# Spreading softmax reciprocals over partitions: by PE matmuls, or through DRAM and by DMA from batch 2 on

## The chip, the cores and the metric

One core of a Trainium2 chip. The time is the device time of one execution in microseconds (us); medians of several executions are given. Engines: PE (matmuls), DVE (vector), ACT (activations), POOL (here it issues the loads) and SP (here it issues output stores, transposes and, in the changed kernel, the row transfers). The 16 DMA engines carry all transfers.

## The reference

Attention over 8 batches, 12 heads, 448 positions, head size 64, then a gated projection pair over the heads' outputs put side by side:

```python
scores = scale * np.matmul(q, k.transpose(0, 1, 3, 2))
scores = scores - np.max(scores, axis=-1, keepdims=True)
attn = np.exp(scores)
attn = attn / (np.sum(attn, axis=-1, keepdims=True) + 1e-09)
attn_out = np.matmul(attn, v)
...  # [batch, heads, seq, 64] -> x [batch * seq, heads * 64]
h = x @ w_in          # 768 x 2048
g = h * np.cos(h)
return g @ w_out      # 2048 x 768
```

## The kernel before

Everything works on transposed tiles: a head's 64 values lie on partitions, its 448 query positions along the free dimension. One step `S` makes scores, `AV` multiplies the exponentials with the values (tile `asb`, not yet normalized), `DN` gets the sums of the exponentials by matmuls with ones (`den`), `N` takes their reciprocals, `R` spreads the reciprocals over the 64 partitions of each head and multiplies, `H` is the first projection (`hps`), `O` the second (`ops`). A sum lies on one partition per head and half of the positions, and it is wanted on 64; `R` does this by a matmul with an indicator matrix:

```python
    def R(ck, b, c):                        # c: one of 3 groups of 4 heads
        ...
        for j in range(2):
            for qh_ in range(2):
                nc.tensor.matmul(rps[j][:, ts(qh_, SH)], ind[:, 2 * c + j, qh_, :, :], rhl[b],
                                 start=True, stop=True)
        ...
        nc.vector.tensor_tensor(out=xt, in0=asb[b, c], in1=both[:, :, 0:S_], op=ALU.mult)
```

The order of PE is fixed when the kernel is built. A planner with a clock of its own (`weave`) takes the next step of the batch if its inputs should be ready, else a step of the next batch ("ahead"), else a piece of the output projection of the batch before ("fill"):

```python
    AHEAD, LATE, KEEP = 3, 6, 8
    ...
        ahead = nxt[: AHEAD if b else 4]
        weave([body, ahead], keep, LATE)
        weave([scaled(b), ahead], keep)                                 # R, R, H, ...
        weave([[(H, b, f2) for f2 in range(2, NFC // 2)]], keep)
        fill += [(O, b, tt, nh, [i, i + 1]) ...]
```

Whenever its buffers should be free, the planner also runs `W`, two DVE copies of the next loaded q and k (which free the load buffer, so POOL starts the next load), and `X`, a DMA transpose of the copy on SP's queue.

The softmax here doesn't subtract the row's maximum and nothing guards it: scores larger than these inputs give would overflow.

Of the kernel before, what the change touches and what calls it, by code (L numbers as in the profile page):

```python
# [11 lines left out]
FP = mybir.dt.float32  # L12
F16 = mybir.dt.float16
AF = mybir.ActivationFunctionType
ALU = mybir.AluOpType
# [56 lines left out]
def kernel(  # L72
# [9 lines left out]
    nc = tc.nc  # L82

    B, NH, S_, D = q.shape
# [17 lines left out]
    sb = ctx.enter_context(tc.tile_pool(name="sb", bufs=2))  # L102
    big = ctx.enter_context(tc.tile_pool(name="big", bufs=1))
    ps = ctx.enter_context(tc.tile_pool(name="ps", bufs=1, space=bass.MemoryType.PSUM))



# [60 lines left out]
    lowrow = const.tile([P, 1], FP, name="lowrow")  # L168
    ind = const.tile([P, NP, 2, 2, D], F16, name="ind")
    halfpi = const.tile([P, 1], FP, name="halfpi")  # L170
    zero = const.tile([P, 512], F16, name="zero")

    def emit_consts_vector():
        nc.vector.memset(zero, 0.0)
# [40 lines left out]
    def take(ck, tag, among=None):  # L215
        return ck.free(tag, among)
# [169 lines left out]
    def DN(ck, b, cs, rs=range(NR)):  # L386
# [16 lines left out]
        for c in cs:  # L403
            for r in rs:
                for h in range(2):
                    for qh_ in range(2):
# [6 lines left out]
                            stop=(c == NQ - 1 and r == NR - 1),  # L413
                        )

    def N(ck, b):
        tag, at = ck.ready["den slot", b]
        ck.slots[tag][at] = ck.on_dve(ck.ready["den", b], 1.5)
        ck.ready["rhl", b] = ck.on_dve(0.0, 0.6)
        if ck is not clk:  # L420
            return
        rr = sb.tile([P, SH], FP, name="rr", tag="rr", bufs=1)
        nc.vector.reciprocal(out=rr, in_=den[b])  # L423
        hi = sb.tile([P, SH], F16, name="hi", tag="hi", bufs=1)
        nc.vector.tensor_copy(out=hi, in_=rr)
        t = sb.tile([P, SH], F16, name="rhl", tag="rhl", bufs=1)
        rhl[b] = t
        nc.vector.scalar_tensor_tensor(
            out=t, in0=hi, scalar=lowrow, in1=rr, op0=ALU.mult, op1=ALU.subtract
        )  # L430

    def R(ck, b, c):

# [38 lines left out]
    def H(ck, b, f2, cs=range(NQ)):  # L472


        if cs[0] == 0:
            ck.ready["hps", f2], t = take(ck, "big", None)
            ck.need(max(t, arrive["win", f2 // 2]))
            if f2 == 0:
                ck.ready["gT slot", b], t = take(ck, "gT", None)
                ck.ready["gT free", b] = t  # L480
        for c in cs:
            ck.need(ck.ready["xT", b, c])
            end = ck.mm("full", 4, 0.189)
        last = cs[-1] == NQ - 1
        at = ck.ready["hps", f2]
        if last:
            if f2 == NFC // 2 - 1:
                for c in range(NQ):
                    ck.slots["xT"][ck.ready["xT slot", b, c]] = ck.pe
            t = ck.on_act(end, 1.0, "sin")  # L490
            t = ck.on_dve(max(t, ck.ready["gT free", b]), 1.09)
            ck.slots["big"][at] = ck.ready["gT", b, f2] = t
        if ck is not clk:
            return
        if f2 == cs[0] == 0:
            gT[b] = big.tile([P, NFC, S_], F16, name="gT", tag=f"gT{ck.ready['gT slot', b]}")
        if cs[0] == 0:
            hpss[f2] = ps.tile([P, 2, 512], FP, name="hps", tag=f"big{at}")
        for i in range(2):
            for kc in range(2 * cs[0], 2 * cs[-1] + 2):  # L500
                nc.tensor.matmul(  # L501
                    hpss[f2][:, i, 0:S_],
                    w_in16[:, kc, ts(2 * f2 + i, P)],
                    xT[b, kc // 2][:, kc % 2, :],
                    start=(kc == 0),
                    stop=(kc == NKC - 1),
                )
        if not last:
            return
        cos = sb.tile([P, 2, S_], FP, name="cs", tag="cs")  # L510
        nc.scalar.activation(out=cos, in_=hpss[f2][:, :, 0:S_], func=AF.Sin, bias=halfpi)  # L511
        nc.vector.tensor_tensor(  # L512
            out=gT[b][:, 2 * f2 : 2 * f2 + 2, :],
            in0=cos,
            in1=hpss[f2][:, :, 0:S_],
            op=ALU.mult,
        )
# [4 lines left out]
    def O(ck, b, tt, nh, fcs):  # L522


        rest = tt == NT
        wait = max(ck.ready["gT", b, fc // 2] for fc in fcs)
        ck.need(max(wait, arrive["wout", 1 if rest else nh]))
        if fcs[0] == 0:
            ck.ready["ops slot"], t = take(ck, "m", None)
            ck.need(t)  # L530
        at = ck.ready["ops slot"]
        end = ck.mm("col64" if rest else "full", len(fcs), 0.1625)
        last = fcs[-1] == NFC - 1
        if last:
            ck.slots["m"][at] = ck.on_act(end, 0.48) if nh == 0 else ck.on_dve(end, 0.556)
            if rest:
                ck.slots["gT"][ck.ready["gT slot", b]] = end
        if ck is not clk:
            return
        gt = gT[b]  # L540
        if fcs[0] == 0:
            opss[0] = ps.tile([P, EH], FP, name="ops", tag=f"m{at}")
        ops = opss[0]
        for fc in fcs:
            for half in (0, 1) if rest else (nh,):
                nc.tensor.matmul(  # L546
                    ops[64 * half : 64 * half + 64, :] if rest else ops,
                    gt[:, fc, ds(P * tt, 64 if rest else P)],
                    w_out16[:, fc, ts(half, EH)],
                    start=(fc == 0),  # L550
                    stop=(fc == NFC - 1),
                )
        if not last:
            return
        osb = sb.tile([P, EH], FP, name="osb", tag="osb", bufs=5)
        (nc.scalar.copy if nh == 0 else nc.vector.tensor_copy)(out=osb, in_=ops)  # L556
        dst = out.rearrange("(b p r) (n e) -> b r n p e", b=B, r=NR, n=2)
        for i in range(2):
            to = dst[b, NR - 1, i] if rest else dst[b, 2 * tt + i, nh]
            nc.sync.dma_start(out=to, in_=osb[SP * i : SP * i + SP, :])  # L560
# [14 lines left out]
    def transpose_ahead():  # L575

        while to_transpose:
            b, c = to_transpose[0]
            now = max(clk.pe, clk.dve)
            if zeros and b > 0:  # L580
                return
            if arrive.get(("qk", b, c), LATER) > now - (1.0 if b and c else 0.0) or min(clk.slots["qkp"]) > now or min(clk.slots["qkT"]) > now:
                return
            to_transpose.pop(0)
            run((W, b, c))
            if b > 1:
                run((X, b, c))
            else:
                soon.extend([(T, b, c, 1), (T, b, c, 0)])

    def weave(lists, keep, late=99):



        body = lists[0]
        while body:
            transpose_ahead()
            waits = []
            todos = ([body, soon] if zeros else [soon, body])
            for todo in todos + (lists[1:] if len(body) <= late else []):  # L600
                while todo and todo[0][0] is N:
                    run(todo.pop(0))
                if todo:
                    w = stall(todo[0])
                    if w <= SLACK:
                        run(todo.pop(0))
                        break
                    waits.append((w, todo))
            else:
                if len(fill) > keep:  # L610
                    waits.append((stall(fill[0]), fill))
                least = min(waits, key=lambda x: x[0])[0] if waits else 1e9
                if zeros and least > 0.15:
                    run((Z,))
                elif least > 1e6:
                    clk.pe += 0.1
                else:
                    run(min(waits, key=lambda x: x[0])[1].pop(0))
# [14 lines left out]

    def scaled(b):

        tail = [(R, b, 0), (R, b, 1), (H, b, 0, [0]), (R, b, 2), (H, b, 0, [1])]
        return tail + [(H, b, 1, [0, 1]), (H, b, 0, [2]), (H, b, 1, [2])]

    LATER = 1e9
    SLACK = 0.02  # L640
    AHEAD, LATE, KEEP = 3, 6, 8
    ctx.enter_context(tc.manual_schedule(engines=None))


# [37 lines left out]
    for b in range(B):  # L682
        nxt = attention(b + 1) if b + 1 < B else []
        ahead = nxt[: AHEAD if b else 4]
        keep = KEEP if b > 0 else 0
        weave([body, ahead], keep, LATE)
        weave([scaled(b), ahead], keep)
        weave([[(H, b, f2) for f2 in range(2, NFC // 2)]], keep)
        halves = [(tt, nh) for tt in range(NT) for nh in range(2)]
        if b == 0:  # L690
            halves.sort(key=lambda x: x[1])
        fill += [(O, b, tt, nh, [i, i + 1]) for tt, nh in halves for i in range(0, NFC, 2)]
        fill += [(O, b, NT, 0, range(i, i + 8)) for i in range(0, NFC, 8)]
        body = ahead + nxt[AHEAD if b else 4 :]
    for step in fill:
        run(step)
# [30 lines left out]
```

## Time and profile before

| | before |
|---|---|
| time, median | 429.27 us (429.02 to 429.66) |
| PE busy | 98% |
| idle notes on PE's timeline, all batches | 3.7 us, all but 0.5 in the first 34 us |
| `rps` matmuls (the spreading) | 96, four per group, 0.385 us a group |

The prediction shows the engine table, the chain and PE's timeline behind one batch's sums. To these belong the longest entries of the list of what PE waited for (engine, line, what ended the wait: us in total, times, longest):

```profile
PE z L229 <- DVE onehot L177: 1.2, 1, 1.2
PE sc L330 <- ACT qkT L299: 1.0, 1, 1.0
PE hps L501 <- DVE xT L463: 0.5, 1, 0.5
```

The steady batches give PE nothing to wait for. The third line, in batch 2, is the only one of a later batch; the three entries left out (0.5, 0.3 and 0.2 us) lie in the first 34 us.

### The profile page before, as it was taken

Reading aid. Unit: us, or ns where it says so; the run is one execution under the profiler, and the core shown is the slowest. Engines: PE = TensorE matmul, PEld = TensorE weight load, DVE = VectorE, ACT = ScalarE, POOL = GpSimd, SP = SyncE. Lnnn points to the kernel's source line nnn. Section 1 sums busy time; section 2 is a strip of 40 time slices with the busy share of each in tenths; the row PEclk is TensorE's granted clock in tenths of the full one; section 3 lists DMA queues with packets and bytes.
Section 4 is the critical chain, followed back from the end, with each engine's and each line's share of the span. In section 5 each row is a group of like instructions: output and inputs, shape, how many; then the busy total and the mean of one; then the engine's idle time right before and its main releaser. Section 6 shows DMA issues by size and latency. Waiting matters only on the chain.

```text
span 427.3 us, 9170 instructions
## 1 busy us (share of the span) xinstructions
PE 419.1 (98%) x4027; PEld 223.8 (52%) x4027; DVE 171.6 (40%) x237; ACT 242.0 (57%) x286; POOL 68.6 (16%) x103
## 2 busy tenths in 40 slices
PE   8989999999999999999999999999999999999995
PEld 3435545655455554655546554555546555565563
DVE  3335633654235542354226442355413542165310
ACT  4898386356755457545774457554575547614300
POOL 7785224101220022100320012100000000000000
PEclk9999999999999999999999999999999999999999
DMA  9999999992996059920999009720364001120033
GB/s 194 191 164 199 204 211 191 163 142 43 177 153 85 0 80 197 127 54 1 137 180 139 2 20 204 149 40 2 73 114 78 20 2 37 40 55 2 18 76 74
DMA packets 68871, 43.12 MB, mean 101 GB/s; under 512 B 36064, under 2 KB 68832, under 8 KB 68832
## 3 DMA queue, kind: packets, MB, share of 16 engines
q0 software_dynamic: 26496, 22.35, 37.2%
q1 hardware_dynamic: 42064, 19.74, 24.9%
q8 instruction: 31, 0.51, 0.5%
q10 hardware_dynamic: 272, 0.46, 0.3%
q14 instruction: 8, 0.07, 0.0%
HBM read 45.61 MB, written 11.01 MB: 133 GB/s over the span
## 4 chain that ended last, share of the span: by engine, by line
PE 88%; DMA 6%; POOL 3%; issue 1%; DVE 1%; ACT 0%; POOLq 0%
PE hps L501 34%; PE ops L546 33%; PE sc L330 8%; PE av L366 7%; DMA win<-in_moe_w_in_dram 4%; PE den L408 3%; DMA out_dram<-osb 2%; PE rps L453 2%; POOL win L155 1%; POOL qkn L133 1%; POOL ind L202 1%; POOL vn L143 1%; DVE osb L556 0%; PE tp L296 0%; ACT osb L556 0%
## 5 line engine op out<-in xcount | busy, mean ns | idle before, releaser
L339 ACT ACTIVATE pT<-sc 128x896 f16<-128x896 f32 x168 | 142.4, 930 | 61.5 <-PE sc L330 61.4
L546 PE MATMUL ops<-wout,gT 128*128 128x384 f16 (+1 forms) x1024 | 162.1, 327 | 0.0
L501 PE MATMUL hps<-xT,win 128*128 128x448 f16 x768 | 148.2, 352 | 0.5 <-DVE xT L463 0.5
L546 PEld LDWEIGHTS <-gT 128*128 128x128 f16 (+1 forms) x1024 | 83.1, 101 | 70.4 <-issue 25.4
L511 ACT ACTIVATE cs<-hps,halfpi 128x896 f32<-128x896 f32 x64 | 63.6, 1006 | 84.3 <-PE hps L501 84.3
L501 PEld LDWEIGHTS <-win 128*128 128x128 f16 x768 | 74.6, 98 | 68.7 <-DVE xT L463 1.6
L512 DVE TENSOR_TENSOR gT<-cs,hps 128x896 f16<-128x896 f32 x64 | 68.9, 1087 | 77.0 <-ACT cs L511 77.0
L378 DVE COPY asb<-av 128x896 f32<-128x896 f32 x23 | 25.1, 1092 | 70.6 <-PE av L366 70.6
L330 PE MATMUL sc<-qkT 64*64 64x448 f16 x672 | 45.5, 359 | 1.0 <-ACT qkT L299 1.0
L556 DVE COPY osb<-ops 128x384 f32<-128x384 f32 x24 | 13.3, 555 | 68.4 <-PE ops L546 53.1
L366 PE MATMUL av<-pT,vn 64*64 64x448 f16 x672 | 38.9, 353 | 0.0
L133 POOL DMA_DIRECT2D qkn<-in_q_dram x23 | 16.6, 723 | 125.6 <-DVE qkp L243 121.9
L143 POOL DMA_DIRECT2D vn<-in_v_dram x24 | 17.2, 717 | 122.1 <-PE av L366 121.0
L556 ACT COPY osb<-ops 128x384 f32<-128x384 f32 x32 | 15.9, 496 | 29.8 <-DMA out_dram<-osb 18.0
L330 PEld LDWEIGHTS <-qkT 64*64 64x64 f16 x672 | 16.2, 105 | 24.2 <-issue 20.3
L463 DVE TENSOR_TENSOR xT<-asb,rps 128x896 f16<-128x896 f32 x21 | 22.2, 1085 | 9.4 <-PE rps L453 9.3
L366 PEld LDWEIGHTS <-vn 64*64 64x64 f16 x672 | 17.6, 106 | 15.1 <-issue 5.9
L408 PE MATMUL den<-pT,onehot 128*32 128x224 f16 x672 | 18.1, 260 | 0.0
L133 POOL DMA_DIRECT2D qkn<-in_k_dram x23 | 16.6, 723 | 6.7 <-DMA wout<-in_moe_w_out_dram 5.3
L408 PEld LDWEIGHTS <-onehot 128*32 128x32 f16 x672 | 15.3, 97 | 3.8 <-issue 3.8
L423 DVE RECIPROCAL rr<-den 128x224 f32<-128x224 f32 x8 | 12.5, 1557 | 11.9 <-PE den L408 11.9
L243 DVE COPY qkp<-qkn 128x896 f16<-128x896 f16 x46 | 15.7, 388 | 0.1
(34 smaller groups left out, 110.9 us busy)
## 6 DMA issues: line engine op xcount, KB each, us to landing
out_dram<-osb SPq DMA_DIRECT2D x112, 96.0 KB, 2.3
vn<-in_v_dram POOLq DMA_DIRECT2D x24, 224.0 KB, 6.3
qkn<-in_q_dram POOLq DMA_DIRECT2D x23, 224.0 KB, 6.6
qkn<-in_k_dram POOLq DMA_DIRECT2D x23, 224.0 KB, 8.9
win<-in_moe_w_in_dram POOLq DMA_DIRECT2D x16, 192.0 KB, 8.3
wout<-in_moe_w_out_dram POOLq DMA_DIRECT2D x2, 1536.0 KB, 19.0
stage<-in_k_dram ACTq DMA_DIRECT2D x1, 448.0 KB, 4.9
stage<-in_q_dram SPq DMA_DIRECT2D x1, 448.0 KB, 4.6
```

What stands on the lines that cost most here:

```text
L133: nc.gpsimd.dma_start(out=t[:, i], in_=rows_of(src, b, c))
L330: nc.tensor.matmul(sc[lo, h, 0:S_], t[64 * h : 64 * h + 64, 1, r, lo], t[64 * h : 64 * h + 64, 0, :, lo], start=True, stop=True,)
L339: nc.scalar.activation(out=pT[b, c][:, r, :, :], in_=sc[:, :, 0:S_], func=AF.Exp, scale=scale)
L366: nc.tensor.matmul(avs[c][64 * h : 64 * h + 64, j, 0:S_], vn[64 * j : 64 * j + 64, h, ts(r, D)], p[64 * j : 64 * j + 64, r, h, :], start=( ...
L378: copy(out=a, in_=avs[c][:, :, 0:S_])
L408: nc.tensor.matmul(den[b][32 * g : 32 * g + 32, :], onehot[:, c, :], pT[b, c][:, r, h, ts(qh_, SH)], start=(c == 0 and r == 0), stop=(c == ...
L463: nc.vector.tensor_tensor(out=xt, in0=asb[b, c], in1=both[:, :, 0:S_], op=ALU.mult)
L501: nc.tensor.matmul(hpss[f2][:, i, 0:S_], w_in16[:, kc, ts(2 * f2 + i, P)], xT[b, kc // 2][:, kc % 2, :], start=(kc == 0), stop=(kc == NKC ...
L511: nc.scalar.activation(out=cos, in_=hpss[f2][:, :, 0:S_], func=AF.Sin, bias=halfpi)
L512: nc.vector.tensor_tensor(out=gT[b][:, 2 * f2 : 2 * f2 + 2, :], in0=cos, in1=hpss[f2][:, :, 0:S_], op=ALU.mult,)
L546: nc.tensor.matmul(ops[64 * half : 64 * half + 64, :] if rest else ops, gt[:, fc, ds(P * tt, 64 if rest else P)], w_out16[:, fc, ts(half, ...
L556: (nc.scalar.copy if nh == 0 else nc.vector.tensor_copy)(out=osb, in_=ops)
```

## The change

Its intent is to take `R` off the busiest engine. From batch 2 on, the reciprocals (fp32) are written to DRAM, and each head's row is read back to all 64 partitions of that head; then DVE multiplies with that (`M`). More work of other batches is kept for the time that this takes, and no new transposes are put on SP's queue shortly before the rows.

```diff
+    BY_DMA = 2
     def N(ck, b):
...
         nc.vector.reciprocal(out=rr, in_=den[b])
+        if b >= BY_DMA:
+            rows = dram.tile([2, 32, 2, SH], FP, name="rows", tag="rows")
+            for h in range(2):
+                nc.sync.dma_start(
+                    out=rows[h].rearrange("m q x -> q m x"), in_=rr[64 * h : 64 * h + 64])
+            for c in range(NQ):
+                rb[b, c] = sb.tile([P, 2, S_], FP, name="rb", tag="cs", bufs=3)
+                for h in range(2):
+                    row = rows[h, 2 * c : 2 * c + 2].rearrange("m q x -> (m q x)")
+                    nc.sync.dma_start(
+                        out=rb[b, c][64 * h : 64 * h + 64].rearrange("p j x -> p (j x)"),
+                        in_=row.unsqueeze(0).to_broadcast([64, 2 * S_]))
+            return
...
+    def M(ck, b, c):
+        nc.vector.tensor_tensor(out=xT[b, c], in0=asb[b, c], in1=rb[b, c], op=ALU.mult)
...
-        osb = sb.tile([P, EH], FP, name="osb", tag="osb", bufs=5)
+        osb = sb.tile([P, EH], FP, name="osb", tag="osb", bufs=4)
...
-            transpose_ahead()
+            if not (body[0][0] in (AV, DN, N) and body[0][1] >= BY_DMA and len(body) <= 3):
+                transpose_ahead()
...
-    AHEAD, LATE, KEEP = 3, 6, 8
+    AHEAD, LATE, KEEP = 5, 7, 28
+    LAND = 8.0
```

Cut: the planner's bookkeeping, its rule that output pieces also fill a wait of over 0.3 us, the new order behind the sums (`M` and one group's part of `H` in turn, then the rest of `H`), the third buffer of tag `cs`, the memory of `zero` shared with another tile, and the half output of a batch as one step in place of two.

More of the change, by code (lines that the diff above doesn't have):

```diff
@@ L104 @@
     ps = ctx.enter_context(tc.tile_pool(name="ps", bufs=1, space=bass.MemoryType.PSUM))
+    dram = ctx.enter_context(tc.tile_pool(name="dram", bufs=2, space=bass.MemoryType.DRAM))
     clk = Clock({"big": 3, "m": 2, "pT": 4, "qkp": 3, "qkT": 4, "asb": 4, "xT": 3, "gT": 2})
@@ L170 @@
     halfpi = const.tile([P, 1], FP, name="halfpi")
-    zero = const.tile([P, 512], F16, name="zero")
+    zero = big.tile([P, 512], F16, name="zero", tag="pT3")
     def emit_consts_vector():
@@ L414, in DN @@
                         )
+    BY_DMA = 2
+    rb = {}
     def N(ck, b):
         tag, at = ck.ready["den slot", b]
-        ck.slots[tag][at] = ck.on_dve(ck.ready["den", b], 1.5)
-        ck.ready["rhl", b] = ck.on_dve(0.0, 0.6)
+        ck.slots[tag][at] = t = ck.on_dve(ck.ready["den", b], 1.5)
+        if b < BY_DMA:
+            ck.ready["rhl", b] = ck.on_dve(0.0, 0.6)
+        else:
+            for c in range(NQ):
+                ck.ready["rb", b, c] = t + LAND + 1.5 * c
         if ck is not clk:
@@ L423, in N @@
         nc.vector.reciprocal(out=rr, in_=den[b])
+        if b >= BY_DMA:
+            rows = dram.tile([2, 32, 2, SH], FP, name="rows", tag="rows")
+            for h in range(2):
+                nc.sync.dma_start(
+                    out=rows[h].rearrange("m q x -> q m x"), in_=rr[64 * h : 64 * h + 64]
+                )
+            for c in range(NQ):
+                rb[b, c] = sb.tile([P, 2, S_], FP, name="rb", tag="cs", bufs=3)
[3 more added lines that the diff above has]
+                        out=rb[b, c][64 * h : 64 * h + 64].rearrange("p j x -> p (j x)"),
+                        in_=row.unsqueeze(0).to_broadcast([64, 2 * S_]),
+                    )
+            return
         hi = sb.tile([P, SH], F16, name="hi", tag="hi", bufs=1)
@@ L430, in N @@
         )
+    def M(ck, b, c):
+        at, t = take(ck, "xT", None)
+        t = max(t, ck.ready["rb", b, c])
+        if ck is not clk:
+            return ck.need(t)
+        ck.ready["xT", b, c] = ck.on_dve(t, 1.09)
+        ck.slots["asb"][ck.ready["asb slot", b, c]] = ck.ready["xT", b, c]
+        ck.ready["xT slot", b, c] = at
+        xT[b, c] = sb.tile([P, 2, S_], F16, name="xT", tag=f"xT{at}", bufs=1)
+        nc.vector.tensor_tensor(out=xT[b, c], in0=asb[b, c], in1=rb[b, c], op=ALU.mult)
     def R(ck, b, c):
@@ L481, in H @@
         for c in cs:
-            ck.need(ck.ready["xT", b, c])
+            ck.need(ck.ready.get(("xT", b, c), LATER))
             end = ck.mm("full", 4, 0.189)
@@ L509, in H @@
             return
-        cos = sb.tile([P, 2, S_], FP, name="cs", tag="cs")
+        cos = sb.tile([P, 2, S_], FP, name="cs", tag="cs", bufs=3)
         nc.scalar.activation(out=cos, in_=hpss[f2][:, :, 0:S_], func=AF.Sin, bias=halfpi)
@@ L609, in weave @@
             else:
-                if len(fill) > keep:
+                least = min(waits, key=lambda x: x[0])[0] if waits else 1e9
+                if len(fill) > keep or fill and least > 0.3:
                     waits.append((stall(fill[0]), fill))
-                least = min(waits, key=lambda x: x[0])[0] if waits else 1e9
+                    least = min(least, waits[-1][0])
                 if zeros and least > 0.15:
@@ L634, in scaled @@
     def scaled(b):
+        if b >= BY_DMA:
+            tail = []
+            for c in range(NQ):
+                tail += [(M, b, c), (H, b, 0, [c])]
+            return tail + [(H, b, 1)]
         tail = [(R, b, 0), (R, b, 1), (H, b, 0, [0]), (R, b, 2), (H, b, 0, [1])]
@@ L686 @@
         weave([body, ahead], keep, LATE)
+        keep = 0
         weave([scaled(b), ahead], keep)
@@ L692 @@
         fill += [(O, b, tt, nh, [i, i + 1]) for tt, nh in halves for i in range(0, NFC, 2)]
-        fill += [(O, b, NT, 0, range(i, i + 8)) for i in range(0, NFC, 8)]
+        fill.append((O, b, NT, 0, range(NFC)))
         body = ahead + nxt[AHEAD if b else 4 :]
```

## The prediction

> **What bounds the kernel now.** I read the page's engine table first, then the chain that ended last, then the PE part of the timeline around one batch's softmax sums, and last the DMA views. The engine table and the chain say the same thing:
>
> ```profile
> PE 419.1 (98%) x4027; PEld 223.8 (52%) x4027; DVE 171.6 (40%) x237; ACT 242.0 (57%) x286; POOL 68.6 (16%) x103
> ...
> PE 88%; DMA 6%; POOL 3%; issue 1%; DVE 1%; ACT 0%; POOLq 0%
> ```
>
> PE is busy for 98% of the span and carries 88% of the chain; the other engines have over 40% to spare. A busy PE need not be a dense one, so I checked the timeline. After batch 2 it shows no idle note on PE at all. A batch is 50.0 us long (the sums of batch 5 end at 277.7 us, those of batch 6 at 327.75). The stretch behind the sums of batch 6 is where the change works:
>
> ```profile
> 325.62 2.20 PE L408 MATMUL den<-pT,onehot 128*32 128x224 f16 x84
> 327.75 1.47 PE L546 MATMUL ops<-wout,gT 128*128 128x384 f16 x8
> 329.15 0.76 PE L330 MATMUL sc<-qkT 64*64 64x448 f16 x12
> 329.85 1.15 PE L546 MATMUL ops<-wout,gT 128*128 128x384 f16 x6
> 330.83 0.55 PE L453 MATMUL rps<-rhl,ind 128*128 128x224 f16 x4
> 331.22 0.49 PE L546 MATMUL ops<-wout,gT 128*128 128x384 f16 x2
> 331.54 0.55 PE L453 MATMUL rps<-rhl,ind 128*128 128x224 f16 x4
> 331.92 0.81 PE L546 MATMUL ops<-wout,gT 128*128 128x384 f16 x4
> 332.57 0.92 PE L501 MATMUL hps<-xT,win 128*128 128x448 f16 x4
> 333.33 0.55 PE L453 MATMUL rps<-rhl,ind 128*128 128x224 f16 x4
> 333.71 17.57 PE L501 MATMUL hps<-xT,win 128*128 128x448 f16 x92
> ```
>
> Columns: start, length, engine, line, operation, tiles, count. The lengths overlap, because matmuls are pipelined; the price of a block is the next start less its own. Three blocks of `rps` (spreading the reciprocals over the partitions of their heads by a matmul) stand between the sums and the first projection `hps`, which starts 4.8 us after the sums. Output matmuls of the batch before fill the wait, and nothing stalls. So a microsecond of PE work taken out of here is a microsecond off the time, as long as no wait takes its place.
>
> **What the Trainium skill says.** "TensorE: Matmul & The Clock Gate", section "Back-to-back issue gap", gives N/2.4 + 2.5 ns for a matmul of N columns at full clock: 96 ns for 224 columns, 0.383 us for the four of a block. The timeline agrees: 331.54 to 331.92 is 0.38, 330.83 to 331.22 is 0.39.
>
> "DMA: Bandwidth & Descriptors", section "Two DMAs through the same engine are not ordered", says that a transfer which reads what an earlier one wrote must be issued after the completion semaphore of the first. So the way through DRAM is two full latencies in series, with the issuing engine waiting between them. The kernel before has no such pair; it shows what one costs:
>
> ```profile
> out_dram<-osb SPq DMA_DIRECT2D x112, 96.0 KB, 2.3
> ...
> vn<-in_v_dram POOLq DMA_DIRECT2D x24, 224.0 KB, 6.3
> ```
>
> (the last number is the median from issue to landing). On a quiet queue, in the stretch from 320 to 345 us, the outputs land in 2.2 us; between 170 and 185 us, with transposes on the same queue and loads beside them, in 9.1. An issue holds SP for 0.59 us (median of 112).
>
> The same page, section "Why a DMA increments its semaphore by 16 and not by 1", says that the slowest dimension of both access patterns sets how many of the 16 engines a transfer uses. The row writes go out with a slowest dimension of 2 on the DRAM side (q, then m, then x), so by that rule each uses only two engines. No run yet shows it.
>
> **The change part by part.**
>
> Removed from PE: blocks of `rps` for six batches, three each, 18 x 0.385 = 6.9 us. One PE wait of the kernel before goes with them, in batch 2:
>
> ```profile
> 132.49 0.93 PE L501 MATMUL hps<-xT,win 128*128 128x448 f16 x4 [0.48 <-DVE xT L463]
> ```
>
> 0.5 us. Together 7.4, and this is the ceiling: nothing else leaves PE. Off DVE go a cast (0.28) and a 0.45 us step in each of six batches, which is worth nothing on an engine that is 40% busy.
>
> Moved on PE: I counted the compiled order of both kernels. PE changes its array mode (full, quarters, columns) 207 times before and 212 times after. In the timeline a block of 6 output matmuls between two other blocks takes 1.08 us (318.25 to 319.33) and one of 12 takes 2.05 (320.02 to 322.07), so one matmul is 0.162 and a change of mode 0.1. Five more are +0.5 us.
>
> Added: a latency, which PE has to cover with other work. By the compiled order, and at the prices of the timeline (8 outputs 1.40, a score block 0.70, 12 outputs 2.05, 28 value matmuls 1.45, 32 half outputs 2.7), PE has this much between the end of the sums and the first `hps`: 12.2 us in batch 2, 12.9 in batches 3 to 6, 9.6 in batch 7, where no next batch is left to draw on (42 outputs and 32 half outputs). The reciprocal ends 1.7 us after the sums (1.56 busy, started 0.12 after them in batch 7). Call that end T0. Then, each figure an estimate from the numbers above:
> - Two row writes: 32 descriptors of 896 B on each of two engines, for each write. In the quiet stretch the hardware queue's 480 packets took 9.6% of 16 engines for 25 us, 80 ns each, mostly of 1536 B; I take 60 ns for 896 B, so 64 x 60 ns = 3.8 us where an output needs 0.3. Second write landed: 2.2 + 3.5 = T0 + 5.7.
> - Two reads of 64 partitions for the first head group, the second issued at T0 + 5.7, then 2.2 and some 0.6 for the larger rows: T0 + 8.5. The other two groups follow at the pace of issue, 2 x 0.6 each: T0 + 9.7 and T0 + 10.9. The change's own plan has 8.0 and 1.5 a group, which is near.
> - A multiply on DVE, 1.09 us by the `xT` row of before, and 0.1 of hand-over: the third group is ready at T0 + 12.1.
>
> The third group is wanted at first `hps` plus 2 x 0.76 us. That is T0 + 12.0 in batch 2 (stall 0.1), T0 + 12.7 in batches 3 to 6 (no stall, 0.6 to spare), T0 + 9.5 in batch 7: a stall of 2.6.
>
> Contention is the part that I can't work out. In batches 2 to 4 loads are still running at that time, and these windows (start and end, length, busy time and count for PE, PEld, DVE, ACT and POOL, PE clock, DMA share, GB/s) say how hard:
>
> ```profile
> 177.70:182.50 4.80, 4.80 (x44) 2.91 (x41) 3.43 (x5) 2.95 (x5) 0.00 (x0) 1.00 1.30 185
> 227.70:232.50 4.80, 4.80 (x44) 2.92 (x40) 3.41 (x5) 2.93 (x5) 0.00 (x0) 1.00 1.09 178
> 277.70:282.50 4.80, 4.80 (x45) 2.92 (x40) 3.39 (x5) 2.91 (x5) 0.00 (x0) 1.00 0.32 48
> ```
>
> The DMA is full behind the sums of batches 3 and 4 and a third used from batch 5 on. Part of this was transposes, which the change keeps from going ahead of the rows. In their place it puts copies on DVE right after the reciprocal that free load buffers, so loads start just then, and it brings 6 x 229 KB of reads per batch itself. The section "Queues, rings and completion order" of the same page has each engine take turns between its queues, so loads would slow the rows, not block them. A delay of 1 us would cost about 1.0 in batch 2 and 0.4 each in 3 and 4, some 1.8 in all; since the plan's 8.0 looks fitted on the chip, I give this 0.5.
>
> Sum: 429.25 - 6.9 - 0.5 + 0.5 + 0.1 + 2.6 + 0.5 = 425.5 us.
>
> **The rivals.**
> First, the latency is hidden everywhere, batch 7 too (writes spread over all 16 engines land in 2.3, not 5.7): then only switches are paid, 429.25 - 7.4 + 0.5 = 422.4. For it: the outputs of the same queue land in 2.3. Against it: the shape of the writes.
> Second, the DMA wait becomes the bound: the loads hold up both hops by 4 us in batches 2 to 4. Then 4.0 + 3.4 + 3.4 of stalls come on top of the 425.0 without contention, 436, slower than before. For it: v loads needed 6.3 us in the median, up to 9.8 in the stretch from 170 to 185, where 3.9 was enough on a quiet machine. Against it: loads and rows are on different queues, and the transposes are gone from the front.
> Third, SP itself: it stands still between writes and reads, outputs queue behind, and their tiles have four buffers in place of five. ACT and DVE copies already waited 33 us on outputs in seven places before, without a PE stall. One PE tile fills in some 2.6 us plus what is woven in, so four buffers cover a 6 us block; I expect nothing from it.
>
> **Range and chances.** The ceiling of 7.4 less the switches makes 422.4 the best that I can build, and 2% faster would be 420.7: 3%, for a price that I missed. 2% slower is 437.8, which needs over 15 us of stalls, more than the second rival: 5%. The rest, 92%, is within 2%. Between rival one and half of rival two the range is 422 to 430.
>
> **What would show it.** `rps` should fall from 96 to 24 matmuls at the same 259 ns. The row writes' median to landing should be 4 to 6 us and the reads' near 3. PE should have an idle note of 2 to 3 us before the `hps` of batch 7, released by the `xT` multiply, and under 1 us in batches 3 to 6. I am wrong if PE idles several microseconds in batches 2 to 4 (contention), if the row writes land in 2.3 (two engines), if batch 7 has no stall, or if PE waits on an output copy or on scores instead.

## The result, and the profile after

450.46 us (448.57 to 451.21) against 429.27: slower. Ratios in this document are the mean time of one kernel's fast runs over that of the other's of the same rounds, so not quite the ratio of the medians quoted; here 1.0486, with a 95% interval of 1.0451 to 1.0522.

The engine table's line for PE and the start of the chain:

```profile
PE 420.9 (94%) x3955; PEld 218.8 (49%) x3955; DVE 168.3 (38%) x225; ACT 242.9 (54%) x286; POOL 68.6 (15%) x103
...
PE 56%; DMA 21%; issue 10%; POOL 4%; SPq 3%; DVE 3%; ACT 1%; DVEq 0%; POOLq 0%; ACTq 0%
```

PE has 72 matmuls fewer and is busy 1.8 us longer; DMA's part of the chain went from 6% to 21%. PE's waits say where:

```profile
PE hps L538 <- DVE xT L467: 18.7, 15, 3.0
PE z L230 <- DVE onehot L178: 1.2, 1, 1.2
```

and the same list for all engines leads from there to the transfers:

```profile
DVE xT L467 <- DMA rb<-rows: 25.3, 16, 4.7
```

The first projection waits 15 times for the normalized tiles, and DVE waits 25.3 us for the rows. On PE's timeline this is batch 3 (start, length, count; in brackets the idle time before a block and what ended it):

```profile
191.01 3.87 PE L583 MATMUL ops<-wout,gT 128*128 128x384 f16 x38
196.57 0.93 PE L538 MATMUL hps<-xT,win 128*128 128x448 f16 x4 [1.69 <-DVE xT L467]
199.17 1.40 PE L538 MATMUL hps<-xT,win 128*128 128x448 f16 x4 [1.67 <-DVE xT L467]
201.89 18.96 PE L538 MATMUL hps<-xT,win 128*128 128x448 f16 x88 [1.32 <-DVE xT L467]
220.69 2.44 PE L583 MATMUL ops<-wout,gT 128*128 128x384 f16 x14
```

and this batch 7, where no loads run any more:

```profile
404.52 0.93 PE L538 MATMUL hps<-xT,win 128*128 128x448 f16 x4 [1.32 <-DVE xT L467]
406.60 0.92 PE L538 MATMUL hps<-xT,win 128*128 128x448 f16 x4 [1.14 <-DVE xT L467]
408.43 16.81 PE L538 MATMUL hps<-xT,win 128*128 128x448 f16 x88 [0.92 <-DVE xT L467]
425.07 18.61 PE L583 MATMUL ops<-wout,gT 128*128 128x384 f16 x128
```

Two things are to be seen. Each of the three head groups comes late, one after the other. And the last 88 matmuls of the projection, which wait for nothing, take 18.8 us in batch 3 (201.89 to 220.69) and 16.6 in batch 7 (408.43 to 425.07). The windows behind the first `hps` of batches 2, 3, 4 and 7 point to the reason; each line has the stretch, its length, busy time and count for PE, PEld, DVE, ACT and POOL, then the granted PE clock, the DMA share and GB/s:

```profile
142.40:164.00 21.60, 20.79 (x96) 9.96 (x97) 9.73 (x9) 8.34 (x8) 0.00 (x0) 0.86 0.48 95
196.50:221.00 24.50, 21.44 (x98) 10.31 (x99) 9.81 (x10) 8.45 (x9) 0.00 (x0) 0.86 0.48 92
252.70:276.00 23.30, 20.23 (x97) 9.94 (x98) 9.81 (x9) 8.33 (x8) 0.00 (x0) 0.93 0.52 93
404.50:425.00 20.50, 18.41 (x96) 9.39 (x97) 9.67 (x9) 8.33 (x8) 0.00 (x0) 1.00 0.20 54
```

The granted clock is down behind the waits of batches 2 to 4. Whether the waits lowered it is tested in e9 below.

The account closes. For each batch I take the time from the end of the sums to the end of the projection, less what PE has to do in it (12.2, 12.95 four times and 9.65 us up to the first `hps`, and 18.17 for its 96 matmuls; both are measured in run e1b below, which has no such wait):

| batch | 2 | 3 | 4 | 5 | 6 | 7 | sum |
|---|---|---|---|---|---|---|---|
| stall expected | 0.1 | 0 | 0 | 0 | 0 | 2.6 | 2.7 |
| lost, measured | 6.5 | 7.7 | 6.2 | 2.4 | 0.9 | 3.8 | 27.5 |
| of it in the last 88 matmuls | 0.8 | 2.2 | 1.6 | 0 | 0 | 0 | 4.6 |

The sum is the difference of the two profiled spans, 448.1 us here and 420.6 in e1b. Which of the two hops came late can be read from DVE and SP; this is batch 3 again:

```profile
181.98 1.56 DVE L433 RECIPROCAL rr<-den 128x224 f32<-128x224 f32 x1 [1.04 <-PE den L409]
183.56 1.11 SPq L437 DMA_DIRECT2D rows<-rr  x2
186.81 4.96 SPq L444 DMA_DIRECT2D rb<-rows  x6
195.42 1.09 DVE L467 TENSOR_TENSOR xT<-asb,rb 128x896 f16<-128x896 f32 x1 [2.67 <-DMA rb<-rows]
```

The first read leaves 3.3 us after the reciprocal's end (186.81 less 183.54). In all six batches it leaves after 3.2 to 3.3 us, and the second read after 4.6 to 5.1, with loads beside it or without, so the loads hardly slowed the writes. What comes late is the reads: the first multiply starts 12.5, 11.9 and 11.4 us after the reciprocal in batches 2 to 4, and 8.2 in batch 7.

### The profile page after: what moved, and what is told of

It reads as the page before. It is cut to its first block, busy times and chain, and to the rows that moved or that the text cites. A ratio compares the mean times of both kernels' runs of the same rounds, so it can differ in the third digit from the quotient of the medians.

```text
span 448.1 us, 9125 instructions
## 1 busy us (share of the span) xinstructions
PE 420.9 (94%) x3955; PEld 218.8 (49%) x3955; DVE 168.3 (38%) x225; ACT 242.9 (54%) x286; POOL 68.6 (15%) x103
## 4 chain that ended last, share of the span: by engine, by line
PE 56%; DMA 21%; issue 10%; POOL 4%; SPq 3%; DVE 3%; ACT 1%; DVEq 0%; POOLq 0%; ACTq 0%
PE hps L538 32%; PE ops L583 15%; DMA rb<-rows 10%; DMA rows<-rr 5%; DMA win<-in_moe_w_in_dram 4%; PE sc L331 3%; PE av L367 3%; SPq L444 3%; DMA vn<-in_v_dram 2%; PE den L409 2%; DVE xT L467 1%; POOL qkn L134 1%; POOL win L156 1%; POOL vn L144 1%; DVE qkp L244 1%
## 5 line engine op out<-in xcount | busy, mean ns | idle before, releaser
L538 PE MATMUL hps<-xT,win 128*128 128x448 f16 x768 | 155.8, 363 | 18.8 <-DVE xT L467 18.7
L583 PE MATMUL ops<-wout,gT 128*128 128x384 f16 (+1 forms) x1024 | 160.4, 327 | 0.0
L538 PEld LDWEIGHTS <-win 128*128 128x128 f16 x768 | 76.2, 100 | 95.8 <-issue 23.2
L379 DVE COPY asb<-av 128x896 f32<-128x896 f32 x23 | 25.1, 1092 | 88.5 <-PE av L367 88.5
L134 POOL DMA_DIRECT2D qkn<-in_q_dram x23 | 16.6, 723 | 144.4 <-DVE qkp L244 141.3
L467 DVE TENSOR_TENSOR xT<-asb,rb 128x896 f16<-128x896 f32 x18 | 19.7, 1092 | 25.3 <-DMA rb<-rows 25.3
L134 POOL DMA_DIRECT2D qkn<-in_k_dram x23 | 16.6, 720 | 6.8 <-DMA wout<-in_moe_w_out_dram 5.2
L433 DVE RECIPROCAL rr<-den 128x224 f32<-128x224 f32 x8 | 12.5, 1558 | 11.9 <-PE den L409 11.9
```

What stands on the lines that cost most here:

```text
L134: nc.gpsimd.dma_start(out=t[:, i], in_=rows_of(src, b, c))
L379: copy(out=a, in_=avs[c][:, :, 0:S_])
L467: nc.vector.tensor_tensor(out=xT[b, c], in0=asb[b, c], in1=rb[b, c], op=ALU.mult)
L538: nc.tensor.matmul(hpss[f2][:, i, 0:S_], w_in16[:, kc, ts(2 * f2 + i, P)], xT[b, kc // 2][:, kc % 2, :], start=(kc == 0), stop=(kc == NKC ...
L583: nc.tensor.matmul(ops[64 * half : 64 * half + 64, :] if rest else ops, gt[:, fc, ds(P * tt, 64 if rest else P)], w_out16[:, fc, ts(half, ...
```

## The experiments

Each is an edit of the changed kernel. "Before" beside them ran at 429.2 to 429.8 us in the median. The changed kernel itself was not run again, so differences from its 450.46 go across sets of rounds. A run counts as slow when it is over 1.5% above the fastest of its kernel; medians are of the fast runs alone, and where there was a slow one the median of all runs is in brackets.

### Is the loss all in the waits? (e1b and e4)

The multiply takes a ready constant; all transfers stay.

```diff
-        nc.vector.tensor_tensor(out=xT[b, c], in0=asb[b, c], in1=rb[b, c], op=ALU.mult)
+        nc.vector.tensor_tensor(out=xT[b, c], in0=asb[b, c],
+                                in1=third.unsqueeze(2).to_broadcast([P, 2, S_]), op=ALU.mult)
```

> The multiply takes a constant 1/448 that is ready from the start in place of the rows from DRAM; all transfers and the order of every engine stay (the result is only nearly right, on purpose). Theory that the 27.8 us lost around the first hps of batches 2 to 7 are waits for the transfers and the slower PE clock behind these waits: no xT wait on PE, PE clock back to about 1.0, and 429.27 - 6.9 - 0.5 + 0.5 = 422.4 us, within 2 us. Rival, that the traffic itself or SP standing still for it costs time through other waits (output copies, scores): still over 435 us.

Measured 422.46 us (422.27 to 422.75), ratio 0.981 (0.975 to 0.987). Batch 3 on PE:

```profile
188.23 18.34 PE L540 MATMUL hps<-xT,win 128*128 128x448 f16 x96
```

One block of 96 with no idle note, 12.95 us after the sums. The saving of the prediction is right to 0.1 us, and all the rest is waiting for the rows and what follows from it.

In e4 the other parts of the change stay and all batches use PE (`BY_DMA = 8`).

> All batches take the PE matmuls, but the other parts of the change stay: the new order (5 steps ahead, 28 fills kept), 4 output buffers, the third cos buffer, the merged half output. If the loss is all in the transfers: 427.5 to 430.5, as the kernel before (208 changes of PE mode against 207). If the new order or the fourth output buffer costs: over 433.

Measured 430.47 (429.89 to 431.94), ratio 1.000 (0.994 to 1.007). The new order and the fourth buffer are not what costs (1.1 us at most, by the medians).

### Loads, writes or bytes? (e2, e3, e10)

e2 keeps `W`, and with it the loads and transposes, from running between the reciprocal and the last multiply of a batch:

```diff
+            held[0] = True           # in N, from batch 2 on
+        held[0] = c < NQ - 1         # in M
-            if not (body[0][0] in (AV, DN, N) and ...):
+            if not held[0] and not (body[0][0] in (AV, DN, N) and ...):
```

> The copies on DVE that free load buffers (and the transposes behind them) are held back from the reciprocal until the last multiply of the same batch, so that no q and k load starts while the rows are on their way. Theory that the loads hold up the rows: batches 2, 3 and 4 lose as batch 5 or 6 does (1 to 2.4 us in place of 6.6, 7.8 and 6.3), the PE clock stays near 1.0, and the time falls by 14 to 18 us to 433 to 437. Rival, that the rows are slow by themselves: under 4 us gained, over 446.

Measured 441.0 (439.46 to 444.08), ratio 1.023 (1.015 to 1.031): 9.5 us less than the changed kernel, well short of what the first theory wanted and more than its rival. The loads matter, and they are not alone. In the profile the first multiply of batch 2 starts 8.8 us after the reciprocal in place of 12.5, and the third still after 13.9 in place of 16.6. The edit holds back the q and k loads and their transposes together, so it doesn't say which of the two weighs more; v loads go on (in batch 3 one is issued at 187.10, among the reads).

e3 writes and reads 16-bit reciprocals:

```diff
+            r16 = sb.tile([P, SH], F16, name="r16", tag="hi", bufs=1)
+            nc.vector.tensor_copy(out=r16, in_=rr)
-            rows = dram.tile([2, 32, 2, SH], FP, name="rows", tag="rows")
+            rows = dram.tile([2, 32, 2, SH], F16, name="rows", tag="rows")
```

(and `rb` likewise).

> The reciprocals go out as 16-bit numbers, so rows and reads have half the bytes; one cast of 0.28 us more on DVE ahead of them. Theory that the reads are bound by bytes (six of 229 KB at the 245 GB/s seen in the quiet batch 7 are 5.6 us): groups come 1 us apart in place of 2, batch 7 loses 1 to 1.5 us in place of 3.8, the contended batches 2 to 3 us less each, together 9 to 13 us less, 437 to 442. Rival, that issue and fixed latencies of the two hops set it: groups still 1.2 us or more apart, batch 7 within 0.7 us of 3.8, over 445 in all.

Measured 432.81 (431.18 to 437.51), ratio 1.007 (0.998 to 1.015), and correct: 17.7 us less, more than expected. In batch 7 the groups come 1.3 and 1.4 us apart in place of 2.1 and 1.8. The writes are halved too, but that gives less: the first read leaves 2.84 us after the reciprocal in place of 3.27. In the changed kernel the stretch of the reads (with output stores beside them from 402.91 on) was bound by the DMA engines, share 1.01 at 242 GB/s; in the same columns as above:

```profile
397.00:398.00 1.00, 1.00 (x8) 0.59 (x7) 0.00 (x0) 0.04 (x1) 0.00 (x0) 1.00 0.14 47
...
402.50:406.00 3.50, 1.63 (x14) 0.63 (x9) 1.64 (x2) 1.76 (x2) 0.00 (x0) 1.00 1.01 242
```

The first of these lines is the row writes of batch 7: a DMA share of 0.14, about two engines of 16 (0.125), as expected from their shape. e10 spreads them:

```diff
-                nc.sync.dma_start(
-                    out=rows[h].rearrange("m q x -> q m x"), in_=rr[64 * h : 64 * h + 64])
+                for q_ in range(2):
+                    nc.sync.dma_start(
+                        out=rows[h, :, q_], in_=rr[64 * h + 32 * q_ : 64 * h + 32 * q_ + 32])
```

> The changed kernel, with each row write cut into two of 32 rows whose slowest dimension is 32, so that 16 engines carry it in place of two; the reads stay. By the profile of the changed kernel the second write lands 4.1 us after its issue, an output 2.3. If two engines are what makes the writes slow: the DMA share during the writes rises, the first group comes some 0.7 us earlier in each batch (four issues in place of two take back part of it), 446 to 448. If issue or the DRAM end sets it: later by an issue or equal, 450 to 453.

Measured 441.75 (fast runs 438.94 to 441.75, one slow at 447.40), ratio 1.024 (1.017 to 1.031): 8.7 us less, about twice the most that was expected (4.5). SP's queue in batch 7 shows the step (start, length until the last issue is done, count). The changed kernel:

```profile
395.19 1.11 SPq L437 DMA_DIRECT2D rows<-rr  x2
398.43 4.43 SPq L444 DMA_DIRECT2D rb<-rows  x6
```

and e10:

```profile
388.33 1.71 SPq L438 DMA_DIRECT2D rows<-rr  x4
390.28 3.96 SPq L445 DMA_DIRECT2D rb<-rows  x6
```

From the first write to the first read 3.24 us, and 1.95 with four writes of half the size, which land in 1.5 us each (median of 24). The second read, which the group needs as well, leaves at 399.82 in the changed kernel, 4.63 us after the first write, and at 391.22 in e10, 2.89 after it. During these writes the DMA share of e10 reaches 0.51 (389.60 to 389.80 us), where that of the changed kernel stays at 0.15 or less from 396.2 to 399.4: they run on more than two engines. By the profiles each batch loses 0.9 to 2.2 us less than in the changed kernel. In five of them the first read leaves 1.2 to 1.3 us earlier; 0.7 had been expected for the first group. In batch 4 it leaves later (3.91 us after the reciprocal), and 1.6 of the 2.1 us less are the clock, which was 1.00 there.

### Does a wait cost a second time? (e9)

Matmuls that nobody reads fill part of PE's waits in batches 2 to 4:

```diff
+        if f2 == 0 and 2 <= b <= 4:
+            for _ in range(20 if cs[0] else 8):
+                lo, hi = (S_, 512) if cs[0] else (0, S_)
+                nc.tensor.matmul(hpss[0][:, 0, lo:hi], w_in16[:, 0, 0:P],
+                                 gT[b - 1][:, 0, 0 : hi - lo], start=not cs[0], stop=not cs[0])
```

> The changed kernel, with idle matmuls (8 of 448 columns ahead of the first group of hps, 20 of 64 columns ahead of each other group, their results never read) in batches 2 to 4, in time in which PE waits for the rows; the transfers stay. Theory that the waits cost a second time because PE's clock is lowered behind them: the clock in the stretches behind the first hps goes from 0.86, 0.86 and 0.93 to near 1.0, the last 88 matmuls of hps there take 16.6 us as in batch 7 in place of 17.5, 18.8 and 18.3, and the time falls by 3 to 5 us to 446 to 448. Rival, that the clock is lowered by something else: it stays under 0.95, and the time stays within 1 us of 450.5 or rises.

Measured 446.63 (fast runs 445.30 to 446.95, one slow at 453.45; median of all runs 446.79), ratio 1.037 (1.030 to 1.043). The windows behind the first `hps` of batches 2 to 4:

```profile
141.43:165.49 24.06, 21.33 (x146) 11.47 (x145) 10.83 (x10) 8.81 (x9) 0.00 (x0) 1.00 0.64 119
196.28:219.18 22.90, 21.17 (x146) 11.48 (x145) 10.83 (x10) 8.81 (x9) 0.00 (x0) 1.00 0.61 114
249.97:273.36 23.39, 21.33 (x146) 11.47 (x145) 10.83 (x10) 8.81 (x9) 0.00 (x0) 1.00 0.61 111
```

The clock is 1.00 in all three, the last 88 matmuls take 16.64 us each time, and the kernel is 3.8 us faster with more work on PE. The mean clock of a whole run was 1.00 in its three fast runs, and 0.98 to 0.99 in the four of the changed kernel. The idle time itself lowered the clock. (The slow run has 0.985; no profile shows why.)

### More time for the rows in place of faster rows? (e6, e11, e7, e8)

e6 changes the planner's constants alone:

```diff
-    AHEAD, LATE, KEEP = 5, 7, 28
-    LAND = 8.0
+    AHEAD, LATE, KEEP = 7, 9, 49
+    LAND = 12.0
```

> Transfers untouched; the planner's constants alone (7 steps ahead, 49 fills kept, landing at 12.0) give PE more other work between the sums and the first hps: by the compiled order 14.1, 18.2, 15.8, 15.8, 15.8 and 14.5 us in batches 2 to 7, in place of 12.2, 12.9 (four times) and 9.6; 204 changes of mode. In the changed kernel the third group came 19.4, 20.0, 19.1, 16.9, 15.4 and 15.0 us after the sums and is wanted 1.5 us after the first hps, so what stays uncovered is 3.8, 0.3, 1.8, 0, 0 and 0 = 5.9 us, on 429.27 - 7.4 - 0.3 = 421.6: 427.5, within 2.5. If SP, output buffers or the clock cost of themselves: over 435.

Measured 439.66 (fast runs 439.19 to 442.77, one slow at 448.44; median of all runs 441.22), ratio 1.026 (1.023 to 1.029): a miss by 12 us. The wait moved. In batch 7, without any load, the rows were there, but DVE stood before an output copy, with the multiplies behind it in the queue:

```profile
394.11 0.56 DVE L593 COPY osb<-ops 128x384 f32<-128x384 f32 x1 [6.89 <-DMA out_dram<-osb]
394.58 0.48 ACT L593 COPY osb<-ops 128x384 f32<-128x384 f32 x1 [4.85 <-PE ops L583]
394.58 3.08 DVE L467 TENSOR_TENSOR xT<-asb,rb 128x896 f16<-128x896 f32 x3
```

The longer window is filled with output tiles, their stores stand behind the rows in SP's order, and four buffers do not last. That is batch 7, where PE lost 1.2 us by it. In all, PE's waits for `xT` fell from 18.7 to 7.6 us, one of 2.8 for another DVE step came in batch 4, and the mean clock was 0.986; the rest of the miss is not traced. e11 is e6 with `bufs=5` there.

> e6 again with five output buffers in place of four. e6 came out at 441 where 427.5 was expected, and its profile has DVE waiting 17 us for output stores that stood in SP's queue behind the rows (three times, up to 6.9). If the missing fifth buffer turned the longer window into that wait: these waits fall to under 6 us and the time by 3 to 6 us, to 435 to 438. If the late rows alone are the cause: within 1.5 us of 441.

Measured 432.71 (431.37 to 435.09), ratio 1.005 (0.998 to 1.013): 7.0 us less than e6, and batch 7 loses nothing. So the buffers were part of it. DVE's waits for stores fell only from 17.0 to 12.5 us, though, and ACT's rose from 5.8 to 14.3; the expectation about the waits was a miss.

e7 is e6 with the half bytes of e3, and e8 is e7 with the loads held as in e2, both with four output buffers.

> The long window of e6 with the half bytes of e3, loads not held. The third groups of e3 came 16.4, 17.7, 16.9 us after the sums in batches 2 to 4 and under 14.5 in the others; uncovered: 0.8 in batch 2, nothing else: 422.4, within 1.5. Theory of hiding: about 1.6% faster than before. Rival, that a longer wait only lets more loads run into the rows: over 425.

Measured 430.28 (fast runs 426.21 to 432.61, one slow at 435.63; median of all runs 430.4), ratio 1.000 (0.996 to 1.004). A miss.

> As e7 and the loads held back too: nothing uncovered, 421.6, within 1.0, if everything is hidden. If it is equal to e7 within 0.5 us, the loads no longer matter once the window is long enough. If held loads come late for the next scores or transposes: slower than e7 by over 1 us.

Measured 424.91 (fast runs 423.46 to 428.59, one slow at 429.92; median of all runs 426.17), ratio 0.995 (0.991 to 0.999): worse than expected. It is better than e7 by 5.4 us in the median, but the intervals of the two ratios overlap, so that loads still matter here is likely and not shown. Both kernels differ from run to run by more than the profile, which caught the fastest run of each, can explain; what the other runs waited for stays open.

### Two and three causes taken away together (e5, e12, e13, e14)

e5 joins e2 and e3 (held loads, half bytes) in the changed kernel's own order; e12 is the same kernel again.

> Loads held back and half the bytes, together. e3 alone still lost 10 us, 9.5 of it in batches 2 to 4, where loads run. If loads and bytes are the two causes, batches 2 to 6 now lose under 0.5 us each and batch 7 0.8 as in e3: 423 to 425. If holding the loads only moves the trouble (e2 lost more in batch 5 than the changed kernel did): over 428.

> The kernel of e5 once more with five rounds, the best so far: 424 to 425.5, 1.0% faster than the kernel before, with an interval that leaves 1 out. A version that beats both, though under the 2% that is called faster.

Measured 424.9 (423.40 to 426.47), ratio 0.990 (0.988 to 0.992), and 423.33 (422.78 to 424.86), ratio 0.984 (0.978 to 0.989). The first is in its range and the second 0.7 us below its own; both are faster than both kernels.

e13 joins e2 and e10 (held loads, spread writes, full bytes).

> Writes spread over 16 engines and loads held back, reads with all their bytes. e2 (held alone) lost 3.0, 4.4, 2.3, 4.5, 0.7 and 5.7 us in batches 2 to 7 of its profile; spread writes start the reads 1.3 us sooner in a quiet batch. If that is all that they do, 1.3 off each that has it: 434, within 2. If the reads' own bytes are the rest: their groups still come some 2 us apart and batches 2 to 5 and 7 still wait for the second and third group. If the writes were the larger part: under 430.

Measured 425.34 (425.02 to 427.24), ratio 0.992 (0.989 to 0.995), where I had expected 434. In its profile batches 2 to 6 lose nothing, and batch 7 loses 2.3 us, with the groups 2.1 and 1.9 us apart. So the bytes of the reads matter by themselves in batch 7 alone.

e14 has all three.

> All three: spread, held, half the bytes. e12 lost 0.9 us in batch 7 and 0.2 in batch 2 of its profile, nothing elsewhere. If the three are the whole of it, nothing is left, and the time is that of e1b, 422.5, within 0.7, the least that taking the matmuls out can give. If a rest of run-to-run waits stays: 423.5 to 425, as e5 and e12.

Measured 422.66 (422.57 to 423.64), ratio 0.985 (0.984 to 0.986), correct: the time of e1b within 0.2 us. PE's line of its engine table:

```profile
PE 412.3 (98%) x3955; PEld 217.2 (52%) x3955; DVE 168.9 (40%) x231; ACT 242.8 (58%) x286; POOL 68.6 (16%) x103
```

PE is at 98% again with 7 us less to do. This version beats both kernels, by 1.5% (under the 2% from which a result is called faster here) and by 6.2% (422.66 / 450.46), the second across two sets of rounds.

| us off the changed kernel's 450.5 | loads as they were | loads held |
|---|---|---|
| as it was | 0 | 9.5 (e2) |
| spread writes | 8.7 (e10) | 25.1 (e13) |
| half bytes | 17.7 (e3) | 25.6, 27.1 (e5, e12) |
| spread and half | not run | 27.8 (e14) |

The effects don't add up, because a wait is only what is left of a delay after PE's other work has covered its part. Held loads or spread writes alone leave the groups late by a piece in most batches; both together bring them inside the 12 to 13 us that PE has anyway.

## Why the prediction was wrong

**Right.** The saving: 6.9 us of matmuls and 0.5 of a wait against 0.5 for the array modes made 422.4 with every wait hidden, and e1b measured 422.46; only the sum of these three was measured. (The page cited for the matmuls gives its formula for one by itself; it is the timeline's 0.38 us that carries the figure.) The windows: 12.2, 12.9 and 9.6 us of other work were expected between the sums and the first `hps`; e1b has 12.20, 12.95 and 9.65. The writes go on two engines. The first group in the quiet batch 7: expected at T0 + 8.5, its multiply started at 403.38, 8.2 us after the reciprocal's end at 395.16. SP, which still issues all the rows in e1b, and the four buffers (e1b and e4) cost nothing in the changed kernel itself; they did when the window was made longer (e6).

**Wrong, a size.** The step "the other two groups follow at the pace of issue, 2 x 0.6 each". They came 2.1 and 1.8 us apart. At the 242 GB/s measured there (output stores in it) a group of 2 x 229 KB takes 1.9. With this the sum gives batch 7 a stall of 4.0 in place of 2.6; 3.8 was lost. A read was given 2.8 us to land (2.2 and 0.6), and the median was 4.2 in batch 7 and 5.7 over all 36. The reads of the first group left earlier than I had them (T0 + 3.3 and T0 + 4.7, not 5.7) and took longer; for that group the two errors cancel, so that it came out right is luck.

**Wrong, the step that failed.** "I give this 0.5": contention was taken as a 1 us delay with a small weight, because the plan's landing time of 8.0 looked fitted. Batches 2 to 4 lost 6.5, 7.7 and 6.2 us in place of 0.6 in all (this 0.5 and the stall of 0.1). The second rival had named the wait and the cause, at a size of 10.8 us and a chance too small; of its two hops only the reads were held up, by 3.2 to 4.3 us before the first multiply (12.5, 11.9 and 11.4 against 8.2), while the first read left after 3.2 to 3.3 us everywhere. Held loads alone gave back 9.5 us (e2), and spread writes alone 8.7 (e10). The change's `LAND` had been read as evidence on the chip; it holds for batch 7's first group (8.2) and for no contended one: in batch 3 the first multiply started 11.9 us after the reciprocal's end (195.42 less 183.54).

**Missing.** The prediction had no term for the clock. The waits lowered it in batches 2 to 4, which cost 4.6 us in the last 88 matmuls there, and e9 got 3.8 back. Batch 5 was taken as quiet and lost 2.4: a v load (issued at 301.5, landing after 7.4 us) and a transpose run beside its reads.

The distribution was too sure: "over 15 us of stalls, more than the second rival" had 5%, and 27.5 us were lost, 22.9 of them apart from the clock.

## What to carry to other kernels

Work that is taken off the busiest engine and put behind a transfer is worth its time only if the whole way of the transfer, under the traffic of that stage, fits into other work; so look at every hop for its width in DMA engines and its bytes, and at what else the change starts at that moment. A landing time written into a scheduler is a hope and not a measurement. When the hops are short and the traffic is moved, the saving that was worked out from the matmuls comes in full.

## What the Trainium skill lacked or had wrong

- "TensorE: Matmul & The Clock Gate", section "HAM oscillation — how this bites in real kernels", gives the rule "no PE-idle gaps >~3.4µs". In batch 3 of the changed kernel no gap before `hps` was over 1.7 us (1.69, 1.67, 1.32, with four matmuls between), and the granted clock was 0.86 over the 24.5 us from the end of the first gap on (0.50 from 200 to 201 us, after the second gap). In batch 7, gaps of 1.32, 1.14 and 0.92 left it at 1.00. So shorter gaps close together can lower the clock, and with most of them filled it stayed at 1.00 in e9. Their length alone doesn't decide: in e2, 0.86 and 1.54 us in batch 3 lowered it (0.92 over 192.3 to 214.9), and 1.79 and 0.90 in batch 2 didn't (1.00). A later section of that page does name frequent short idles between groups of matmuls, without lengths.
- "DMA: Bandwidth & Descriptors", section "Why a DMA increments its semaphore by 16 and not by 1", is right on two engines for a slowest dimension of 2 (share 0.14). It doesn't say what that costs: here 1.3 us from the first write to the first read in a quiet batch and 1.7 to the second, and 8.7 us of the kernel over six batches (e10).
- No page looked up gives a rate for one DRAM row read to 64 partitions: 229 GB/s at a DMA share of 0.88 in batch 7 (402 to 403 us), and 242 at 1.01 with the first output stores beside it (402.5 to 406).
